# A new order for the 1224 steps of a fused gated-mix kernel

## The chip, the cores and the metric

The kernel runs on one core of a Trainium2 chip. The metric is the time of one execution on the device, in microseconds (us). The kernel before was timed in three runs; their median is the time before.

## The reference

The input x has 2048 rows of 512 float32 values. Two branches work on it and a gate mixes them:

```python
x = A_x
g = _sigmoid((x * gate_w).sum(-1, keepdims=True))
a = _A_ref(x, A_wqkv, A_w_phi, A_wo)
b = _B_ref(x, B_w1, B_b1, B_w2)
return g * a + (1 - g) * b
```

Branch A is linear attention with 32 heads of width 16. From `x @ wqkv` come q, k and v. Per head, q and k are multiplied by `w_phi`, and the feature map is the softmax of the product beside the softmax of its negative. `kv` is the sum over rows of (features of k) times v, `z` the sum over rows of the features of k. The output of a head is `num / den`, with `num` the features of q times `kv` and `den` the features of q times `z`, and the joined heads are multiplied by `wo`:

```python
phi_k = jnp.concatenate([_softmax(pk, axis=-1), _softmax(-pk, axis=-1)], axis=-1)
kv = jnp.einsum("bhsf,bhsd->bhfd", phi_k, v)
z  = jnp.einsum("bhsf->bhf", phi_k)
num = jnp.einsum("bhqf,bhfd->bhqd", phi_q, kv)
den = jnp.einsum("bhqf,bhf->bhq", phi_q, z)[..., None] + 1e-6
```

Branch B is a dense layer of width 1376 with a Mish activation, `h * tanh(softplus(h))`, and a second dense layer back to 512.

## The kernel before

Three kinds of work, by the letter that begins a step's name. **A0 to A7** are eight chunks of 256 rows: the projections to q, k and v, the features of k, and the sums `kv` and `z`. **S0 and S1** are two halves of 1024 rows of the first dense layer: five pairs of 128 hidden columns each (`_0` to `_4`) and one last group (`uf0`, `uf1`). **B0 to B3** are four blocks of 512 rows: the features of q, `num` and `den`, the second dense layer (`dn0` to `dn10`, `df`), the product with `wo`, the mix, and the output.

Every float32 factor is split into a high and a low part, so that a product is three matmuls, and one step named `h`, `hi`, `wa`, `wc`, `gh` or `xh` (ScalarE writes the high part) goes before a step named `o`, `lo`, `wb`, `wd`, `gl` or `xl` (GpSimd, or VectorE for three of the S halves' parts, subtracts to get the low part).

The v and q projections of chunks A1 to A7 and the five pairs of S0 and S1 use a scheme with seven products in the place of eight. It ties the engines together in a chain on PSUM banks. `p1` opens bank a; `c1` (ScalarE) copies it out; `p6` adds to the same bank, so it has to wait until `c1` has read it; `c6` copies again, `p7` adds, `a7` (VectorE) reads, `p4` adds, and `mA1` or `e4` (ScalarE) reads the end. `p5` opens bank b, `c5` (ScalarE) copies, `p3` adds, `a3` (VectorE) reads. `p2` opens bank c, `a2` (VectorE) reads it. Each `p` is six matmuls of 128x512. There are 17 such groups (seven chunks, ten pairs), and so 68 places where a product waits until the copy of what its bank held before has been read out: `p1` to `p6`, `p6` to `p7`, `p5` to `p3` and `p7` to `p4`.

```python
            def p6():
                product(ps["a"], sv(0, 0), Xv("2"))
...
            def copy(n, b):
                v[n] = k2("act", "hl")
                act(v[n], ps[b])
```

PSUM has eight banks in three rings: three of tag `a` (the helper `psum`, line 133), four of tag `dn`, one of tag `kv`. A step that opens a bank waits until the last reader of the bank's earlier tenant is done. Buffers in SBUF are shared in the same manner by tag.

The order of all steps is written out: `RUN` is a text of 1224 names, and `run` (line 218) calls the functions of each name in turn. Every instruction is pinned (`tc.keep_in_program_order`), so each engine and each DMA queue gets its instructions in the order in which `RUN` names their steps; between engines only semaphores order the work. A step that issues a load or a store puts it on the queue of SyncE (SP), apart from the running sums `z` of branch A, which are accumulating DMAs that GpSimd issues, and one half of the last output, which ScalarE issues. The queue of SP is in order too: a store that waits for its data holds back every load named behind it.

ScalarE holds one table of functions at a time. Exp (steps `E`, `ge`) and Mish (steps `mA0` to `mB1`, `mi0`) are in different tables, so each change from one to the other in the order of ScalarE costs an ACT_TABLE_LOAD; copies need none.

The last steps of the kernel are `fi0` to `fi3` of B3. `fi3` is split: the function `rest` (line 1038) makes the last two groups of columns of row tile 3 in two halves of 256, and stores each half on a queue of its own.

Lines that the prediction names: 118 (all matmuls), 138 (all of ScalarE's activations), 285 and 287 (the two subtractions ahead of an exp, steps `d0` and `d1`), 740, 743 and 746 (`a2`, `a3`, `a7` of the pairs), 954 (`T`, the product of the features of q with `z`), 958 (`D`, its sum), 700 (`wd`), 824 (`lo`), 559 (`gl`), 549 (the loads `lg` of the second layer's weights), 1050 and 1061 (the additions that finish an output tile).

Of the kernel before, what the change touches and what calls it, by code (L numbers as in the profile page):

```python
# [46 lines left out]
    A0.st0 A0.st1 A0.z1 A1.c6 A0.z0 A1.z0 S0.h21 A2.c1 A1.p5 A0.kv A1.c5 A1.S1 A1.rS1 A1.p7 A1.p3 A2.sh A2.sl A3.su A2.mn0 A1.ml1 A1.a7 A2.mx1 A1.st1
    A3.k1 A2.a2 A1.a3 A2.mx0 A2.d10 A2.d00 A3.p1 A2.E0 A2.S0 A3.ldx A2.rS0 A1.z1 S0.wr_0 A2.p6 A2.c6 A2.ldx A2.p5 A2.c5 A2.p7 A1.p4 A2.d01 A2.mn1
    A2.d11 A2.E1 A2.p3 A3.sh S0.wa_0 A2.ml0 A1.st0 A3.mn1 A3.c1 A3.k0 A2.a3 A2.z0 A2.st0 A3.sl A3.p5 A2.a7 A2.p4 A1.e4 A3.xh A2.S1 A3.mx0 A3.mx1
    A3.mn0 A1.kv A3.xl S0.l12 A2.e4 A2.rS1 A2.ml1 A2.kv A3.d00 A3.d10 A3.E0 S0.wb_0 S0.ws_0 A3.p6 A4.p1 A2.z1 A3.d11 A3.S0 A3.rS0 A3.ml0 A2.st1 A2.wx  # L50
    A3.c5 A4.k0 A4.mn0 A3.c6 A4.su A3.p3 A4.d10 A3.a3 A4.c1 A3.p7 A4.sh A4.mx0 S0.h11 A4.d00 A3.a7 A4.k1 A4.E0 A3.st1 A3.d01 A4.mn1 A4.d11 A4.S0 A4.sl
    A3.p2 A3.a2 A4.mx1 A4.p5 A4.p6 A3.z0 A3.E1 A4.xh A4.c6 A4.ldx A3.S1 A3.rS1 A4.p2 A4.p7 A4.d01 A4.c5 A3.ml1 A3.p4 A4.a7 A4.st1 A4.E1 A3.st0 S0.o11
    A4.xl A4.rS0 A4.ml0 A4.p3 A5.su A5.sh A4.a3 A3.z1 S0.t1 A3.e4 B0.lq0 A5.k0 A5.k1 A5.mx0 A4.S1 A4.z0 A4.rS1 A4.ml1 A5.sl S0.h1 S0.o1 A4.z1 S0.o21
    A5.xh A5.p1 A5.c1 A3.kv A5.p5 A5.c5 A4.st0 A4.a2 A5.mn0 A5.p6 A5.mx1 A5.xl A5.d01 S0.wc_0 A5.mn1 A5.d10 A5.d11 A5.d00 A5.E0 A4.p4 A5.S0 A5.rS0
# [20 lines left out]
    B0.iz2 B0.ol0 B1.S1 B0.iz0 B0.iz1 B0.wo0 B1.mi0 B1.hi0 B1.lo0 B0.iz3 B0.wo1 B1.S0 B1.rS0 B1.m0 B1.la4 B1.hc B1.la5 B1.hi1 B1.dn0 B1.mn3 B1.rS1
    B0.nu1 B1.T1 B1.de0 B1.d03 B1.D1 B1.m1 B1.d13 B1.de1 B1.d02 B1.lo1 B1.E3 B1.d12 B0.fi0 B1.rd0 B1.sc0 B1.es0 B1.cd B2.lq0 B1.hi3 B1.lo3 B0.oh1
    B1.dn1 B1.rd1 B0.ol1 B0.wo2 B1.sc1 B1.E2 B1.es1 B1.S2 B1.hi2 B1.lo2 B1.hi4 B1.lo4 S1.l11 B1.tr1 B1.dn2 B2.lq1 S1.h11 S1.o11 B1.hi5 B1.la6 B1.lo5
    S1.t1 B1.dn3 B1.dn4 B1.tr0 B1.hi6 B1.la7 B1.hi7 B0.fi2 B1.lo6 B1.rS2 B2.mx0 B1.S3 B1.la9 B0.wo3 B1.lo7 B1.T2 B1.mv0 B1.D2 B1.dn5 B1.dn6 B1.dn7
    B1.m2 B1.nu0 B1.rS3 B1.T3 B1.D3 B1.m3 B1.la8 B1.gl B1.de2 B1.ge B1.de3 B1.rd2 B1.sc2 B1.rd3 B1.es2 S1.l22 B1.sc3 B1.es3 B1.hi8 B1.lo8 B0.fi1 S1.h1
    S1.t3 S1.o1 B1.dn8 B1.gg B1.oh0 B1.tr2 B2.mx1 B1.hi9 B1.la10 B1.tr3 S1.h3 B1.lo9 B0.fi3 S1.h22 B1.ol0 B1.wo1 B1.wo0 S1.o22 B1.hi10 B1.lo10 B1.mv1  # L80
    S1.o3 B1.dn9 B1.nu1 B1.ag1 B1.df2 B1.ag0 S1.wr_0 B2.mn1 S1.t2 B2.d11 B2.d01 B2.E1 S1.wa_0 S1.fr0 B1.oh1 B2.lq2 S1.fh0 B2.S1 B1.ol1 B1.df1 S1.h2
    B1.df0 S1.wb_0 S1.p1_0 S1.c1_0 S1.ws_0 S1.wc_0 B2.d00 S1.o2 S1.l21 S1.h21 S1.wd_0 S1.o21 B2.mn0 B2.d10 B1.wo3 B1.ag3 B1.wo2 S1.fl0 S1.t4 S1.p6_0
    S1.wr_1 S1.p5_0 S1.c6_0 B2.mn2 B2.d12 B1.df3 B1.fi3 B2.rS1 B1.fi1 S1.p2_0 B2.mx2 B1.ag2 S1.a2_0 S1.wr_2 S1.c5_0 S1.p3_0 S1.p7_0 S1.a3_0 B2.E0
    B2.S0 S1.wa_1 S1.wb_1 S1.p1_1 S1.ws_1 S1.h4 S1.mB0_0 S1.o4 S1.wc_1 S1.c1_1 S1.wd_1 B1.fi0 S1.uf0 S1.a7_0 S1.p2_1 S1.p4_0 B2.rS0 S1.a2_1 B1.fi2
    B2.gr S1.p5_1 B2.mi0 B2.hi0 S1.p6_1 S1.mA0_0 B2.gl B3.lq1 B2.lo0 S1.mA0_1 B2.hc B2.dn0 B2.mn3 S1.sB0_0 B2.hi1 B2.mx3 B2.d02 B2.T0 S1.c6_1 B2.T1
    B2.D1 B2.m1 B2.de1 S1.wa_2 B2.rd1 B3.lq0 S1.p7_1 S1.mB1_0 S1.wb_2 S1.p1_2 S1.mA1_0 S1.sB1_0 B2.D0 B2.cd B2.d03 S1.c5_1 S1.p3_1 B2.E2 B2.ge B2.lo1
# [1148 lines left out]
```

## Time and profile before

| | |
|---|---|
| three runs | 435.71, 430.99 and 432.29 us |
| median | 432.29 us |
| span of the profiled execution, first to last instruction | 431.1 us |
| TensorE (PE) busy | 422.3 us, 98% |
| VectorE (DVE) busy | 369.3 us, 86% |
| ScalarE (ACT) busy | 253.6 us, 59% |
| GpSimd (POOL) busy | 263.6 us, 61% |
| mean granted clock of TensorE | 0.996 |

The profiled execution has no time of its own beside its span; the fastest of the three runs (430.99 us) is within 0.2 us of that span, so little lies around it. In the profile, a line such as L118 is a line of the kernel, `out<-in` names the tiles that an instruction writes and reads, `x12` is a count, and what stands in brackets behind a row of the timeline is the idle time of that engine before it and what ended it. A busy PE is not a PE at its peak, since the ends of matmuls are modelled; the rate is read from the starts.

### The profile page before, as it was taken

Reading aid. Unit: us, or ns where it says so; the run is one execution under the profiler, and the core shown is the slowest. Engines: PE = TensorE matmul, PEld = TensorE weight load, DVE = VectorE, ACT = ScalarE, POOL = GpSimd, SP = SyncE. Lnnn points to the kernel's source line nnn. Section 1 sums busy time; section 2 is a strip of 40 time slices with the busy share of each in tenths; the row PEclk is TensorE's granted clock in tenths of the full one; section 3 lists DMA queues with packets and bytes.
Section 4 is the critical chain, followed back from the end, with each engine's and each line's share of the span. In section 5 each row is a group of like instructions: output and inputs, shape, how many; then the busy total and the mean of one; then the engine's idle time right before and its main releaser. Section 6 shows DMA issues by size and latency. Waiting matters only on the chain. (4 is left out here: it accounts for less than half of the span.)

```text
span 431.1 us, 7558 instructions
## 1 busy us (share of the span) xinstructions
PE 422.3 (98%) x2772; PEld 340.2 (79%) x2772; DVE 369.3 (86%) x519; ACT 253.6 (59%) x373; POOL 263.6 (61%) x186
## 2 busy tenths in 40 slices
PE   8999999999998999899999999999999999999996
PEld 7888888888886877688878687788788887877875
DVE  3899789998998999998999998799989699999512
ACT  3574463646254899768679813467978467851131
POOL 2298868799674966635666494977455627541220
PEclk9999999999999999989999999999999999999999
DMA  7900597675988344433888477833533725555532
GB/s 260 366 34 28 164 273 182 140 179 126 209 171 214 108 134 123 160 109 122 235 249 281 165 239 237 281 91 122 177 119 143 232 73 188 179 199 168 197 121 75
DMA packets 52670, 74.06 MB, mean 172 GB/s; under 512 B 8085, under 2 KB 32149, under 8 KB 52633
## 3 DMA queue, kind: packets, MB, share of 16 engines
q1 hardware_dynamic: 50440, 66.36, 47.9%
q0 software_dynamic: 1904, 6.82, 9.5%
q8 instruction: 22, 0.36, 0.3%
q10 hardware_dynamic: 288, 0.39, 0.3%
q14 instruction: 16, 0.12, 0.1%
HBM read 43.53 MB, written 28.85 MB: 168 GB/s over the span
## 5 line engine op out<-in xcount | busy, mean ns | idle before, releaser
L118 PE MATMUL down<-w2g,h 128*128 128x512 f32 x316 | 98.5, 393 | 0.0
L118 PEld LDWEIGHTS down<-w2g,h 128*128 128x128 f32 x316 | 58.6, 188 | 14.8 <-issue 2.5
L118 PE MATMUL down<-w2g,l 128*128 128x512 f32 x158 | 61.8, 391 | 0.2 <-POOL l L824 0.2
L824 POOL TENSOR_TENSOR l<-act,h 128x512 fp32r<-128x512 f32 (+1 forms) x24 | 32.3, 1345 | 41.2 <-ACT h L138 16.7
L824 POOL TENSOR_TENSOR l<-actb,h 128x512 fp32r<-128x512 f32 x20 | 29.0, 1451 | 38.3 <-ACT h L138 20.7
L138 ACT ACTIVATE E<-E 128x1024 f32<-128x1024 f32 x32 | 33.4, 1057 | 16.5 <-DVE E L285 7.1
L118 PE MATMUL up<-x,w1sh 128*128 128x512 f32 x144 | 39.7, 397 | 2.2 <-DVE act L740 2.1
L118 PE MATMUL wo<-woh,ohl 128*128 128x512 f32 x128 | 40.9, 389 | 0.0
L118 PEld LDWEIGHTS down<-w2g,l 128*128 128x128 f32 x158 | 29.6, 188 | 7.5 <-POOL l L824 1.2
L118 PEld LDWEIGHTS up<-x,w1sh 128*128 128x128 f32 x144 | 26.7, 189 | 9.2 <-DVE act L740 2.5
L700 POOL TENSOR_TENSOR w1sl<-w1r,w1sh 128x1024 fp32r<-128x1024 f32 x9 | 22.2, 2467 | 18.0 <-ACT w1sh L138 17.4
L118 PE MATMUL proj<-tw,sx 128*128 128x512 f32 x126 | 31.5, 394 | 1.5 <-ACT qs L138 1.5
L628 POOL TENSOR_TENSOR x<-xr,x 128x1024 fp32r<-128x1024 f32 x10 | 26.7, 2666 | 3.6 <-ACT x L138 3.6
L118 PEld LDWEIGHTS proj<-tw,sx 128*128 128x128 f32 x126 | 23.3, 188 | 6.9 <-ACT qs L138 1.9
L138 ACT ACT_TABLE_LOAD x22 | 28.2, 1283 | 0.4
L118 PEld LDWEIGHTS wo<-woh,ohl 128*128 128x128 f32 x128 | 24.0, 188 | 5.0
L138 ACT ACTIVATE act<-act,b1s 128x512 f32<-128x512 f32 x30 | 21.4, 719 | 10.9 <-DVE act L740 4.1
L118 PE MATMUL up<-x,w1d 128*128 128x512 f32 x108 | 27.7, 398 | 0.0
L267 POOL TENSOR_TENSOR xl<-xraw,xh 128x512 fp32r<-128x512 f32 x14 | 18.3, 1370 | 15.3 <-ACT xh L138 15.0
L138 ACT ACTIVATE act<-up 128x512 f32<-128x512 f32 x30 | 17.6, 590 | 16.8 <-PE up L118 16.4
L138 ACT ACTIVATE h<-actb 128x512 fp32r<-128x512 f32 x20 | 12.4, 628 | 24.4 <-DMA actb<-ab 18.9
L118 PE MATMUL wo<-wol,ohl 128*128 128x512 f32 x64 | 24.9, 389 | 0.0
(173 smaller groups left out, 1086.4 us busy)
## 6 DMA issues: line engine op xcount, KB each, us to landing
ed<-E SPq DMA_DIRECT2D x16, 512.0 KB, 3.1
eT<-ed SPq DMA_DIRECT2D x64, 128.0 KB, 3.2
za<-E POOLq DMA_DIRECT2D x11, 512.0 KB, 6.8
xr<-in_xT_dram SPq DMA_DIRECT2D x20, 256.0 KB, 4.2
ab<-act SPq DMA_DIRECT2D x20, 256.0 KB, 2.9
actb<-ab SPq DMA_DIRECT2D x20, 256.0 KB, 3.3
pqd<-qs SPq DMA_DIRECT2D x16, 256.0 KB, 5.8
pq<-pqd SPq DMA_DIRECT2D x16, 256.0 KB, 3.6
```

Source lines behind the costliest of these rows:

```text
L118: return pin(nc.tensor.matmul(*a, **k))
L138: return pin(A_.activation(out_, in_, fn, **k))
L267: pin(eng.tensor_sub(xs[c][1][j], kt(rawx[c], SC)[:, 2 * j : 2 * j + 2, :], f32(xs[c][0][j])))
L628: pin((V if n in LOV else G_).tensor_sub(X[n][:, 1024:], xr[n], f32(X[n][:, :1024])))
L700: pin(G_.tensor_sub(W["sl"], W["r"], f32(W["sh"])))
L824: pin(G_.tensor_sub(U[i]["l"][:n, :], U[i]["a"][:n, :], f32(U[i]["h"][:n, :])))
```

## The change

The text `RUN` is replaced by another with the same 1224 names in another order. No function, tile, size or instruction changes. What moves is the place of each step in the queue of its engine, the place of each DMA in its queue, and with the order of first use also which buffer and which bank a tile gets. The names are in groups on lines that have no meaning. The lines that the prediction speaks of:

```diff
--- before.py
+++ after.py
 RUN = """
-    A0.mx0 A0.mx1 A0.xh A0.xl A0.v0 A0.mn1 A0.mn0 A0.fq A0.fh2 S0.l11 A0.d10 A0.tA0 A0.fh1 A0.v1 A0.tA1 A0.tH1 A0.fl1 A0.tB1 A0.tB0 A0.fl2 A1.p1
...
-    A6.ml1 S0.h2 S0.t3 S0.fh0 S0.t4 A7.k0 S0.h22 A6.z1 S0.fl0 S0.o22 A6.e4 A7.mn0 A6.a3 A5.kv A6.kv A7.c1 S0.lg1 A7.d10 A7.mx0 A7.d00 B0.d00 A6.zm
-    S0.o2 A7.p5 A7.E0 A7.S0 A7.rS0 A6.st0 A7.c5 A7.k1 A7.mx1 A7.mn1 S0.gh1 S0.gl1 S0.wr_1 S0.h3 S0.p1_0 A7.d01 A7.p6 A7.c6 A7.d11 A7.p3 A7.ml0 A7.E1
...
-    B0.d12 B0.dn2 S0.wd_2 B0.T0 B0.hi3 B0.D1 B0.lq3 S0.c1_2 S0.p6_2 S0.mB1_1 B0.rS0 B0.E2 B0.D0 S0.wa_3 B0.lo3 S0.sB1_1 S0.a2_2 B0.rS1 B0.m1 B0.mx3
-    S0.p4_1 S0.mA1_1 B0.hi4 S0.lg2 S0.c6_2 B0.de1 S0.wr_4 B0.dn3 S0.gl3 S0.wb_3 S0.mA0_2 S0.p5_2 S0.p1_3 S0.lg4 S0.c5_2 S0.a3_1 B1.lq0 S0.gh4 B0.lo4
...
-    B0.hi6 S0.wc_4 B0.tr0 B0.lo6 B0.dn6 S0.mB1_3 S0.sB1_2 S0.wd_4 S0.a3_3 S0.mA1_3 S0.mB0_3 S0.sB0_3 B0.T3 B0.D3 B0.S3 B1.d00 B1.lq1 S0.gl4 B0.rS3
-    S0.c1_4 B0.hi7 B1.mn0 B1.d10 S0.p6_4 S0.c6_4 B0.m2 S0.p5_4 B0.mv0 S0.p7_4 B0.de2 B0.lo7 S0.c5_4 B1.E0 B0.gg S0.h12 S0.fr1 B0.m3 B0.de3 S0.p2_4
...
-    B3.hi9 B3.lo9 B3.dn8 B3.de2 B3.rd2 B3.hi10 B3.sc2 B3.lo10 B3.es2 B3.tr3 B3.tr2 B3.mv1 B3.df1 B3.fi1 B3.nu1 B3.oh1 B3.df2 B3.ol1 B3.wo2 B3.ag2
-    B3.fi2 B3.wo3 B3.ag3 B3.df0 B3.fi0 B3.fi3
+    A0.xh A0.mn0 A0.mx1 A0.d01 A0.v0 A0.fq A0.fh1 A0.mn1 A0.d11 A0.ve0 A0.xl A2.lx A0.tA0 A0.tA1 A0.ldx A0.tH1 A0.tL1 A0.mx0 A0.d00 A0.fl1 A0.v1 A0.tB1
...
+    A6.rS1 A6.ml1 A6.z0 A5.kv S0.o1 A6.p5 A6.c5 A6.p7 A6.p3 A6.a7 S0.l22 S0.t3 A6.zr A6.z1 A7.sh A7.sl S0.lg1 A6.a3 A6.st0 A7.k0 S0.wc_0 A7.mn0 A7.d10
...
+    A7.p5 A7.k1 A7.mx1 A7.mn1 A7.d01 S0.gh1 S0.gl1 A7.p6 A7.c5 A7.p3 S0.h22 A7.d11 A7.c6 A7.p7 S0.o22 A7.E1 A7.a2 S0.fl0 S0.wr_1 S0.wa_1 S0.p1_0 S0.c1_0
...
+    A7.zt B0.d03 S0.p5_1 B0.hi0 B0.lo0 B0.dn0 S0.c5_1 S0.p3_1 S0.wb_2 S0.p2_2 B0.mn1 S0.mA1_0 B0.hi2 S0.lg3 S0.gh3 B0.lo2 A7.st1 S0.wr_3 A7.zf S0.c6_1
+    B0.gl B0.ge B0.mx1 B0.d01 S0.ws_2 B0.d11 B0.lq2 B0.mn2 B0.mx2 S0.wc_2 S0.p7_1 B0.E1 S0.a7_1 A7.zs S0.wa_3 A7.zl B1.lq3 S0.wr_4 S0.p1_2 S0.c1_2
+    S0.lg2 S0.a3_1 B0.dn3 S0.mB1_1 B0.dn2 S0.a2_2 S0.mA0_2 S0.p4_1 S0.wd_2 S0.p5_2 S0.mB0_1 S0.mB1_0 S0.sB1_0 S0.wb_3 S0.p6_2 B0.d13 B0.T0 B0.D0
...
+    B1.mx0 B0.E3 S0.wd_4 S0.p5_4 S0.mA0_3 S0.mB0_3 S0.sB0_3 B1.mn0 B0.S3 S0.c1_4 B1.d00 S0.p6_4 B0.T3 B0.D3 S0.p4_3 B0.hi7 B1.d10 S0.ldo1 B0.lo7 B0.rS3
+    B0.dn7 B0.S2 S0.gh4 B0.rS2 B0.m2 B0.de2 B0.rd2 S0.o12 B1.E0 B1.T0 B1.D0 S0.a2_4 S0.c6_4 S0.p7_4 S0.mA1_3 B0.hi8 S0.fr1 B0.lo8 B1.lq1 B1.mn1 B1.d11
+    S0.c5_4 S0.p3_4 S0.gl4 B0.dn8 S0.fh1 S0.fl1 B0.m3 B0.de3 B0.rd3 S0.mA0_4 B0.hi9 S1.l11 S1.h11 S0.ldo0 S0.mB1_3 S0.sB1_3 S0.a7_4 S0.mB1_4 S0.sB1_4
...
+    B3.ol0 B3.wo0 B3.hi7 B3.lo7 B3.dn7 B3.la9 B3.hi9 B3.ge B3.gg B3.wo1 B3.ag1 B3.la10 B3.hi10 B3.lo10 B3.cd B3.nu1 B3.dn8 B3.oh1 B3.ol1 B3.ag0 B3.wo3
+    B3.ag3 B3.lo9 B3.df0 B3.fi0 B3.df1 B3.fi3 B3.fi1 B3.wo2 B3.df2 B3.ag2 B3.fi2
 """
```

More of the change, by code (lines that the diff above doesn't have):

```diff
@@ L47 @@
[L47 to L54, printed above, removed]
@@ L75 @@
[L75 to L82, printed above, removed]
@@ L83 @@
[L83 to L86, printed above, removed]
@@ L91 @@
-    S1.ws_4 B2.rS3 B2.rS2 S1.wd_3 S1.p6_3 S1.h12 S1.c6_3 S1.fr1 S1.mA1_2 B2.lo5 S1.wc_4 S1.wd_4 B2.dn5 B2.hi6 S1.p5_3 S1.c5_3 S1.p7_3 B2.m3 S1.p1_4
-    S1.c1_4 B2.de3 B2.rd3 S1.a7_3 B2.lo6 S1.ldo0 B2.gg B3.d01 B2.hi7 B3.d11 S1.p3_3 S1.fh1 B2.T2 S1.a2_4 S1.mA0_4 B2.dn6 B3.d10 B3.mx0 S1.p6_4 S1.c6_4
-    B2.lo7 S1.p4_3 S1.fl1 B2.D2 B2.m2 B3.E1 B3.d00 B2.sc3 B2.de2 B2.rd2 B3.E0 B2.sc2 B3.lq2 B2.es2 S1.mA1_3 B2.dn7 S1.p5_4 S1.c5_4 B2.es3 S1.p7_4
-    B3.mn2 S1.ldo1 B2.hi8 S1.p3_4 B2.tr2 B3.S1 S1.WH1 S1.a3_4 S1.mB0_4 B2.lo8 B2.dn8 S1.o12 S1.mB1_3 B3.mn3 S1.sB0_4 S1.sB1_3 B2.hi9 B2.lo9 S1.a7_4
@@ new lines @@
+    B1.d02 B1.E2 B1.d03 B1.hi3 B1.lo3 B1.la2 B1.hi4 B1.lo4 B1.dn3 B2.lq0 B1.sc0 B1.es0 B1.T1 B1.D1 B1.hi2 B0.fi0 B1.tr0 B1.m1 B1.de1 B1.rd1 B1.gl B1.ge
+    B1.dn4 B1.sc1 B1.T2 B1.la7 B0.oh1 B1.S2 B1.es1 B1.tr1 B1.lo2 B1.dn2 B1.d13 B1.D2 B0.ol1 B1.E3 B0.wo3 S1.o11 B1.hi7 S1.t1 B1.rS2 S1.h1 B2.mn1 B0.wo2
+    B1.lo7 B1.dn7 B1.S3 B1.rS3 B1.la8 B1.m2 B1.de2 B1.rd2 B1.sc2 B1.T3 B1.la6 B1.la9 B1.hi9 B1.D3 B1.m3 B1.lo9 B1.dn9 B1.mv0 B1.hi5 B1.lo5 B1.dn5 B1.hi6
+    B1.lo6 B1.hi8 S1.l22 S1.h22 B1.de3 B1.rd3 B1.sc3 B1.es2 B1.tr2 B0.fi2 B1.es3 B1.tr3 B2.mx1 B2.d01 B1.dn6 S1.t3 S1.h3 B1.lo8 B2.mx0 S1.o3 B1.nu0
@@ new lines @@
+    S1.wd_1 B2.d12 B2.lq3 S1.o4 S1.p4_0 B2.hi0 B2.lo0 B2.mx3 S1.wr_2 B1.fi2 B2.S0 B1.fi1 S1.c1_1 S1.p6_1 B2.mx2 B2.gr S1.wr_3 S1.a2_1 B1.fi3 S1.p5_1
+    S1.c6_1 S1.p7_1 S1.wa_2 S1.wb_2 S1.ws_2 S1.c5_1 S1.p3_1 S1.mA0_0 S1.mA1_0 S1.p2_2 B2.hc S1.wc_2 S1.a3_1 B2.T0 B2.d02 B2.D0 B2.dn0 S1.a7_1 S1.p1_2
+    B2.hi1 B2.lo1 B2.dn1 B2.d03 B2.hi2 B2.lo2 B2.dn2 B2.E2 B2.T2 B2.D2 B3.lq0 B3.mn0 S1.mB1_1 S1.wa_3 S1.wd_2 S1.c1_2 S1.p6_2 S1.c6_2 B3.mx0 S1.a2_2
+    S1.mA0_2 S1.p5_2 S1.mB0_1 S1.sB0_1 B2.rS0 B2.m0 S1.mA0_1 B2.hi3 S1.p7_2 B2.mn3 B2.d13 B2.de0 S1.wb_3 S1.sB1_1 S1.p4_1 S1.c5_2 S1.p3_2 S1.ws_3 B2.T1
@@ new lines @@
+    B2.sc2 B2.es2 S1.fr1 B3.d11 B3.E1 B2.tr2 S1.p3_3 S1.a3_3 B3.lq2 B3.T1 S1.p6_4 B2.lo7 S1.c6_4 S1.p5_4 B2.dn7 B2.rS3 B2.m3 B2.de3 B2.rd3 S1.mB0_3
+    S1.sB0_3 B2.hi9 S1.p7_4 B2.lo9 S1.fh1 S1.fl1 B3.d00 B3.E0 S1.o12 B2.sc3 B2.es3 S1.p4_3 B2.dn9 B3.S1 B3.rS1 B2.tr3 S1.c5_4 S1.p3_4 S1.a7_4 S1.p4_4
+    S1.mB1_4 S1.sB1_4 B3.mn3 B3.D1 B3.m1 B3.de1 B3.S0 B3.la1 S1.ldo0 S1.WH1 S1.WL1 B3.rS0 B3.mx3 B3.T0 B3.D0 B3.m0 B3.de0 B2.gg S1.mA1_3 B2.hi8 S1.mA1_4
+    B2.lo8 B3.d13 B3.hi1 B3.lo1 B2.hi10 B2.lo10 S1.WH0 S1.uf1 B2.cd B2.nu0 B2.oh0 B2.ol0 B2.mv1 B2.dn8 B2.dn10 B2.iz0 B2.iz2 B3.la6 B3.gr B3.rd1 B3.mn2
@@ new lines @@
+    B3.d12 S1.a3_4 S1.mB0_4 S1.sB0_4 B3.la5 B3.mi0 B3.hc B3.la2 B3.la3 B3.rd0 B3.sc0 B3.es0 B3.tr0 B2.iz1 B3.la4 B3.d03 B3.mx2 B3.d02 S1.WL0 B2.wo0
+    B2.fi0 B3.sc1 B3.es1 B2.nu1 B3.tr1 B3.mv0 B3.E3 B3.S3 B2.wo1 B2.iz3 B2.oh1 B3.dn1 B2.ol1 B2.wo2 B2.fi2 B3.E2 B3.T2 B3.hi0 B3.lo0 B3.hi5 B3.dn0 B3.D2
+    B3.S2 B3.rS2 B3.m2 B3.de2 B3.rd2 B3.hi3 B3.lo5 B2.wo3 B2.fi3 B3.dn5 B3.lo3 B3.dn3 B3.T3 B3.hi2 B3.nu0 B3.lo2 B3.la7 B3.gl B3.dn2 B3.la8 B3.hi4
+    B3.lo4 B3.dn4 B3.hi6 B2.fi1 B3.hi8 B3.lo6 B3.dn6 B3.D3 B3.rS3 B3.m3 B3.sc2 B3.es2 B3.tr2 B3.de3 B3.rd3 B3.sc3 B3.lo8 B3.es3 B3.tr3 B3.mv1 B3.oh0
```

59 lines of the change are left out of this document (32 added, 27 removed).

## The prediction

> **What bounds the kernel now.** I read the page first, for the share of each engine; then the waits of TensorE; then stretches of time around the longest of them; then the queues that were late there.
>
> ```profile
> span 431.1 us, 7558 instructions
> PE 422.3 (98%) x2772; PEld 340.2 (79%) x2772; DVE 369.3 (86%) x519; ACT 253.6 (59%) x373; POOL 263.6 (61%) x186
> ```
>
> TensorE is busy for 422.3 of 431.1 us, and an order takes no matmul away. The chain that ended last has its rate:
>
> ```profile
> 312.57 2.72 PE down L118 x12
> ```
>
> Twelve matmuls of 128x512 start in 2.72 us, 0.227 us each, so one product `p` of six is 1.36 us and a step `dn` of twelve 2.72 us. The 8.8 us without a busy TensorE are its start, its end, and these waits:
>
> ```profile
> PE up L118 <- DVE act L740: 2.1, 1, 2.1
> PE proj L118 <- ACT qs L138: 1.5, 1, 1.5
> ...
> PE up L118 <- POOL w1sl L700: 0.3, 1, 0.3
> ...
> PE down L118 <- POOL l L824: 0.2, 1, 0.2
> ```
>
> Together 4.1 us, all behind the prologue and so within reach of a new order. The longest cost more than itself. By stretches around it (length, then busy time and count of PE, PEld, DVE, ACT, POOL, then the granted clock):
>
> ```profile
> 180.40:182.50 2.10, 0.02 (x2) 0.01 (x1) 2.10 (x4) 1.99 (x5) 1.11 (x2) 1.00 0.32 104
> 182.50:184.50 2.00, 2.00 (x6) 1.62 (x7) 1.97 (x5) 0.69 (x1) 0.82 (x1) 0.64 0.82 209
> 184.50:186.50 2.00, 2.00 (x7) 1.51 (x6) 2.00 (x6) 0.92 (x2) 0.00 (x0) 0.51 0.84 311
> ```
>
> After 2.1 us of idleness the clock was 0.64 and then 0.51: 2 x 0.36 + 2 x 0.49 = 1.7 us lost. So 4.1 + 1.7 = 5.8 us is all that better waits can bring, 1.3% of the span.
>
> [...]
>
> **The change part by part.** Both texts have the same 1224 names, so sums of work by engine stay, but for table loads (below). All steps are pinned to the text's order, so that nothing happens at all isn't a case.
>
> *The wait of 1.5 us (A7, `p6` to `p7`).* ScalarE, then TensorE:
>
> ```profile
> 137.87 0.64 ACT L138 ACTIVATE w2g<-raw 128x512 fp32r<-128x512 f32 x1 [4.12 <-DMA raw<-in_w2a_dram]
> 138.40 1.04 ACT L138 ACTIVATE x<-xr 128x1024 fp32r<-128x1024 f32 x1
> 139.53 0.60 ACT L138 ACTIVATE qs<-proj 128x512 f32<-128x512 f32 x1
> 140.18 1.66 PE L118 MATMUL proj<-tw,sx 128*128 128x512 f32 x6 [1.52 <-ACT qs L138]
> raw<-in_w2a_dram SPq DMA_DIRECT2D x6, 256.0 KB, 7.4
> ```
>
> `gh1` stood ahead of `A7.c6` in ScalarE's queue and waited 4.1 us for the load `lg1`. Loads of this kind land 7.4 us after their issue (median), and between the names `lg1` and `gh1` stand only 4.1 us of matmuls before; after the change 11.9 us (`A7.k0`, `k1` and more between). I count this wait as gone: -1.5. SP's queue isn't free of the reverse: `lg3` had 15.7 us ahead of `gh3` and has none now, and `gh3` is followed by `c6_1`. What hides it is that `p6_1` and `p7_1`, which need that copy, stand 5.9 us apart; without that cover it would cost up to 4.1 us, as above.
>
> *The wait of 2.1 us (`p5_2`).* VectorE's queue ahead of it:
>
> ```profile
> 176.86 2.31 DVE L954 TENSOR_TENSOR T<-E,zb 128x1024 f32<-128x1024 f32 x1
> 179.10 1.21 DVE L958 TENSOR_REDUCE Dn<-T 128x64 f32<-128x1024 f32 x1
> ...
> 180.69 1.15 DVE L958 TENSOR_REDUCE Dn<-T 128x64 f32<-128x1024 f32 x1
> 181.77 0.67 DVE L740 TENSOR_TENSOR act<-up,act 128x512 f32<-128x512 f32 x1
> ```
>
> `a2_2`, which frees the bank, stood behind `T0`, `D1` and `D0` of block B0, about 4.7 us of work. In the new text it follows `a3_1` at once, `T0` and `D0` come behind it, and five steps of matmuls stand between `p2_2` and `p5_2`. Gone, with its clock: -3.8. The waits of 0.3 and 0.2 us I count as gone too: -0.5.
>
> *The banks of the seven-product groups.* What is new is how close `p6`, `p7`, `p3` and `p4` stand behind the product whose copy they wait for. Of the 68 places, 10 had a single product (1.36 us) between before; now 25 have. What such a place leaves over is seen in chunk A4, where `p6`, `p2`, `p7` follow each other:
>
> ```profile
> 82.16 1.52 PE L118 MATMUL proj<-tw,sx 128*128 128x512 f32 x6
> ...
> 83.72 1.09 ACT L138 ACTIVATE qs<-proj 128x512 f32<-128x512 f32 x2 [2.25 <-PE proj L118]
> ...
> 84.88 0.84 PE L118 MATMUL proj<-tw,sx 128*128 128x512 f32 x3
> ```
>
> `p6` ends at 83.68, the copy begins at 83.72, takes 0.6 (two overlapped ones 1.09) and ends at about 84.3; `p7` starts at 84.88, in turn and unhurried. About 0.5 us is left: a ScalarE that is free holds the pace, one that is 0.6 us late does not. Of the 10 places before, one was late, by 1.5 us. The same share of 25 would be 2.5 places, 3.75 us; none late is 0. The cause of the one was a late load ahead of the copy, which got a longer lead, and the five close places of `p7` to `p4`, which wait for VectorE, all lie in the A chunks, where its operations read one operand from PSUM and keep their time (rows below). I take one late place: +1.5, with 0 and 3.75 as ends.
>
> *A pile on ScalarE (`c1_4` to `c5_4`).* Table loads rise from 22 to 24 by the order of Exp and Mish, 2.6 us on an engine that is 59% busy: hidden, except where they pile up ahead of a copy. Between `c1_4` and the end of `c5_4` the new text has `hi7`, `gh4` (two), a table load, `E0` of B1, `c6_4`, a table load, `mA1_3`, `hi8` and `c5_4` itself:
>
> ```profile
> L138 ACT ACTIVATE E<-E 128x1024 f32<-128x1024 f32 x32 | 33.4, 1057 | 16.5 <-DVE E L285 7.1 <-PE proj L118 5.3 <-DVE E L287 3.4
> L138 ACT ACT_TABLE_LOAD x22 | 28.2, 1283 | 0.4
> L138 ACT ACTIVATE act<-act,b1s 128x512 f32<-128x512 f32 x30 | 21.4, 719 | 10.9 <-DVE act L740 4.1 <-DVE act L746 4.0 <-DVE act L743 2.5
> L138 ACT ACTIVATE act<-up 128x512 f32<-128x512 f32 x30 | 17.6, 590 | 16.8 <-PE up L118 16.4 <-ACT h L138 0.4
> L138 ACT ACTIVATE h<-act 128x512 fp32r<-128x512 f32 (+2 forms) x28 | 17.6, 627 | 2.3 <-DMA ab<-act 1.3 <-PE down L118 0.7
> ```
>
> In the same sequence, with 0.64 for each `gh`: 0.63 + 1.28 + 1.28 + 1.06 + 0.59 + 1.28 + 0.72 + 0.63 + 0.59 = 8.1 us, or 7.3 with the overlap of 0.1 between neighbours. TensorE has `p6_4`, `p4_3`, `dn7` and `p7_4` in that time: 1.36 + 1.36 + 2.72 + 1.36 = 6.8 us, then `p3_4` needs `c5_4`. The wait is 0.5 us if `c1_4` ends as `p6_4` begins, 1.3 without overlap, 0 if ScalarE runs ahead by half a us. I take +0.6.
>
> *The end.* Before, the last product was split:
>
> ```profile
> 427.74 0.48 DVE L1050 SCALAR_TENSOR_TENSOR io<-rest,og_sb,io 128x256 f32<-128x256 f32 x1 [0.23 <-PE rest L118]
> 426.34 0.74 DVE L1061 SCALAR_TENSOR_TENSOR io<-down,og_sb,io 128x512 f32<-128x512 f32 x1
> out_dram<-io SPq DMA_DIRECT2D x15, 256.0 KB, 2.3
> out_dram<-io ACTq DMA_DIRECT2D x1, 128.0 KB, 1.7
> ```
>
> Now `fi3` with its halves lies ahead of `wo2`, and the kernel ends with `df2`, `ag2`, `fi2`: an addition of full width, 0.74 in place of 0.48, and a store of 256 KB, 2.3 in place of 1.7: +0.9 (0.3 if the store lands as fast as the half did). `ag2` (one copy on ScalarE) is hidden under `df2`, 1.36 us.
>
> **The sum.** 431.1 - 5.8 + 1.5 + 0.6 + 0.9 = 428.3 us for the profiled execution. It stands 1.2 below the median of the three runs; the runs differ by their waits, and part of these go, so I carry half of it over: 428.3 + 0.6 = 428.9, said as 429.0 us, 0.8% under the median.
>
> **The rivals.** *All waits go and the close places hold.* 431.1 - 5.8 + 0.9 + 0.6 (carried over) = 426.8 us. For it: nine of ten close places held. Against it: the place at `p3_4`, and 15 more close places.
>
> *VectorE's backlog comes back elsewhere.* It is busy for 86% and its operations are the same. Then the wait of 2.1 us and its clock return at another place; only 1.5 + 0.5 go: 431.1 - 2.0 + 0.6 + 0.9 = 430.6, with the whole 1.2 431.8 us. No change that can be measured. For it: VectorE was busy for all of the 2.1 us in which TensorE waited (2.10 of 2.10 in the first stretch). Against it: freeing steps now stand ahead of the long ones.
>
> *Long operations fall ahead of close places: slower.* A VectorE operation that reads two operands from SBUF lengthens beside GpSimd:
>
> ```profile
> 169.39 2.50 POOL L700 TENSOR_TENSOR w1sl<-w1r,w1sh 128x1024 fp32r<-128x1024 f32 x1 [0.31 <-PE up L118]
> 169.55 3.43 DVE L954 TENSOR_TENSOR T<-E,zb 128x1024 f32<-128x1024 f32 x1
> L287 DVE TENSOR_TENSOR E<-mn,pq 128x512 f32<-128x512 f32 x16 | 18.5, 1158 | 0.1
> L287 DVE TENSOR_TENSOR E<-mn,proj 128x512 f32<-128x512 f32 x16 | 10.8, 681 | 0.2
> ```
>
> The same subtraction takes 1158 ns from SBUF (`pq`) and 681 from PSUM (`proj`), and `T` beside a GpSimd operation of 2.50 took 3.43, 2.2 more than the 1.21 of `D`, an operation of its width. Which one is lengthened changes with the neighbours, so an order whose copies fit by half a us can be late wherever a long pair now falls: through an exp that waits for a lengthened subtraction, or a Mish that waits for a late `a2`, ScalarE's queue stops, and the copy behind it. Each such place costs 2.2 - 0.5 = 1.7 us. The time is over 1% above the median from 436.6 - 426.8 = 9.8 us on, six late places of 25; seven give 426.8 + 11.9 = 438.7 us. Against it: before, two lost more than 1 us in the whole kernel.
>
> [...]
>
> **How the numbers follow.** The forecast has 0.38, with 427 to 431 as its own range (close places between 0 and 3.75, the pile 0 to 1.3). All waits gone 0.28; the backlog elsewhere 0.15; slower 0.19. About 1% is what a measurement of this kernel can tell from no change, below 428.0 or above 436.6 us. Faster: 0.26 of the 0.28 and 0.10 of the forecast's 0.38, 0.36. Slower: 0.18 of the 0.19. The same: the rest, 0.46. The range of 8 in 10 goes from 425.5, a little under the case with all waits gone, since the three runs scatter, to 434.5, which takes in the forecast, the backlog, and the slower case up to three or four late places.
>
> **What would show it.** The waits of TensorE have no row of `up` for VectorE's L740 over 1 us and none of `proj` for ScalarE over 1; the mean clock rises from 0.996 to 1.0. Rows of `up` or `proj` for ScalarE of 0.3 to 1.5 us appear, one of them at `p3_4` around 205 to 210 us. The span ends some 4.3 us behind the start of the first operation after the last matmul, in place of 3.4 (431.1 - 427.74). I am wrong if TensorE's idle time after the prologue is more than 5 us, or if a wait of 2 us brings the half clock back.

## The result, and the profile after

The new order is slower by 5.7%: 457.26 us (median of four runs, 455.5 to 459.8) beside 431.64 for the kernel before on the same chip, a ratio of 1.057 (95% interval 1.051 to 1.064). The forecast was 429.0 us. The ratios, here and below, leave out the slowest executions of a kernel and so differ a little from the ratio of two medians. The profiled execution took 459.8 us, 1.7 more than its span. Every execution of the runs below takes 1.7 to 2.1 us more than its span too, so the span of 431.1 us before stood for some 432.8 us, near the median, and not for the fastest run.

The page of after, its busy times:

```profile
span 458.1 us, 7542 instructions
...
PE 427.5 (93%) x2772; PEld 339.7 (74%) x2772; DVE 396.8 (87%) x519; ACT 256.3 (56%) x375; POOL 266.4 (58%) x186
```

The span grew by 27.0 us. TensorE does the same 2772 matmuls in 5.2 us more and is now without work for 30.6 us in place of 8.8. VectorE does the same 519 instructions and needs 27.5 us more for them (396.8 for 369.3). ScalarE and GpSimd need under 3 us more.

What TensorE waited for in after (total, times, longest):

```profile
PE up L117 <- ACT act L137: 7.6, 5, 2.3
PE wo L117 <- DVE ohl L1011: 5.7, 4, 1.8
PE up L117 <- DVE act L745: 4.7, 3, 1.7
PE up L117 <- DVE act L739: 2.0, 1, 2.0
PE proj L117 <- ACT qs L137: 1.7, 1, 1.7
PE kvp L117 <- DVE E L301: 1.3, 1, 1.3
...
PE down L117 <- POOL l L823: 0.9, 1, 0.9
```

Lines stand one lower than before. By steps these are 19 waits with 24.8 us, from `A3.p3` at 76 us to `B2.wo2` at 410, the longest 2.3. Two are followed by half clock, each for 3.4 us, which loses 1.7 us each time. Here is the first of the two, by stretches as in the prediction:

```profile
187.00:189.00 2.00, 1.65 (x7) 1.38 (x8) 2.00 (x2) 1.86 (x4) 1.11 (x1) 0.95 0.19 73
189.00:191.00 2.00, 2.00 (x7) 1.54 (x6) 2.00 (x2) 0.00 (x0) 2.00 (x2) 0.50 0.00 0
```

VectorE's own groups, shapes apart, first before and then after:

```profile
L285 DVE TENSOR_TENSOR E<-pq,mx 128x512 f32<-128x512 f32 x16 | 15.8, 986 | 0.1
L285 DVE TENSOR_TENSOR E<-proj,mx 128x512 f32<-128x512 f32 x16 | 10.8, 682 | 0.4 <-PE kvp L118 0.2
L962 DVE SCALAR_TENSOR_TENSOR den<-Dn 128x32 f32<-128x32 f32 x16 | 4.2, 267 | 0.2
L854 DVE COPY zr<-zr 32x32 f32<-32x32 f32 x3 | 0.5, 171 | 0.1
```

```profile
L284 DVE TENSOR_TENSOR E<-pq,mx 128x512 f32<-128x512 f32 x16 | 22.1, 1389 | 0.2
L284 DVE TENSOR_TENSOR E<-proj,mx 128x512 f32<-128x512 f32 x16 | 11.0, 685 | 0.2
L961 DVE SCALAR_TENSOR_TENSOR den<-Dn 128x32 f32<-128x32 f32 x16 | 8.6, 536 | 0.4
L853 DVE COPY zr<-zr 32x32 f32<-32x32 f32 x3 | 2.7, 897 | 0.0
```

The subtraction that reads PSUM (`proj`) is as long as before. The same one from SBUF (`pq`) grew, and so did even operations that are 32 columns wide. Single rows of after:

```profile
189.14 2.81 POOL L699 TENSOR_TENSOR w1sl<-w1r,w1sh 128x1024 fp32r<-128x1024 f32 x1
189.65 2.38 DVE L976 TENSOR_TENSOR Dn<-Dn,Sm 128x64 f32<-128x64 f32 x1
...
216.57 2.40 POOL L627 TENSOR_TENSOR x<-xr,x 128x1024 fp32r<-128x1024 f32 x1
216.65 2.87 DVE L284 TENSOR_TENSOR E<-pq,mx 128x512 f32<-128x512 f32 x1
...
222.54 1.06 ACT L137 ACTIVATE E<-E 128x1024 f32<-128x1024 f32 x1 [5.01 <-DVE E L286]
223.50 0.58 ACT L137 ACTIVATE act<-up 128x512 f32<-128x512 f32 x1
...
224.13 0.74 PE L117 MATMUL up<-x,w1sh 128*128 128x512 f32 x2 [1.94 <-ACT act L137]
```

and the same two steps (`B0.m0`, `B1.d00`) before:

```profile
184.88 0.16 DVE L977 TENSOR_TENSOR Dn<-Dn,Sm 128x64 f32<-128x64 f32 x1
...
210.28 0.68 DVE L285 TENSOR_TENSOR E<-pq,mx 128x512 f32<-128x512 f32 x1
```

A product of 64 columns took 2.38 us in place of 0.16, ending just behind a GpSimd operation. `B1.d00` took 2.87 in place of 0.68; the exp behind it kept ScalarE waiting for 5.0 us, of which 2.2 are this lengthening, and the copy `c6_4`, queued behind that exp, let TensorE wait for 1.9 us at `p7_4`. Counted over all of VectorE's instructions, against the lower quartile of like ones in both traces, 34 are more than 0.2 us too long before and 47 after, and only 10 steps are among both. The excess is 32 us before and 55 after. So the length of such an operation goes with what GpSimd does at that moment and not with the step, and the lengths seen in the order of before didn't carry over to the new one.

The tail: the last addition starts at 454.19, the span ends 3.9 us later (3.4 before).

```profile
454.19 0.75 DVE L1060 SCALAR_TENSOR_TENSOR io<-down,og_sb,io 128x512 f32<-128x512 f32 x1 [3.02 <-ACT io L137]
```

### The profile page after: what moved, and what is told of

The parts are those of the page before. It is cut to its first block, busy times and chain, and to the rows that moved or that the text cites. A ratio compares the mean times of both kernels' runs of the same rounds, so it can differ in the third digit from the quotient of the medians.

```text
span 458.1 us, 7542 instructions
## 1 busy us (share of the span) xinstructions
PE 427.5 (93%) x2772; PEld 339.7 (74%) x2772; DVE 396.8 (87%) x519; ACT 256.3 (56%) x375; POOL 266.4 (58%) x186
## 4 chain that ended last, share of the span: by engine, by line
PE 48%; DVE 34%; issue 7%; POOL 5%; DMA 3%; ACT 2%; SPq 1%; DVEq 0%; POOLq 0%; ACTq 0%
PE proj L117 21%; PE down L117 10%; PE up L117 7%; PE wo L117 6%; DVE T L953 3%; DVE E L301 3%; DVE Dn L957 2%; DVE E L284 2%; DVE Sm L290 2%; DVE E L286 2%; DVE Dn L976 2%; DVE E L968 2%; DVE den L961 2%; DVE mn L274 1%; PE kvp L117 1%
## 5 line engine op out<-in xcount | busy, mean ns | idle before, releaser
L117 PEld LDWEIGHTS down<-w2g,h 128*128 128x128 f32 x316 | 59.6, 190 | 14.7 <-issue 2.3
L823 POOL TENSOR_TENSOR l<-act,h 128x512 fp32r<-128x512 f32 (+1 forms) x24 | 36.1, 1504 | 57.4 <-ACT h L137 39.0
L823 POOL TENSOR_TENSOR l<-actb,h 128x512 fp32r<-128x512 f32 x20 | 30.3, 1516 | 39.2 <-ACT h L137 18.3
L117 PE MATMUL wo<-woh,ohl 128*128 128x512 f32 x128 | 42.2, 395 | 5.8 <-DVE ohl L1011 5.7
L117 PEld LDWEIGHTS up<-x,w1sh 128*128 128x128 f32 x144 | 26.5, 188 | 14.3 <-ACT act L137 8.4
L699 POOL TENSOR_TENSOR w1sl<-w1r,w1sh 128x1024 fp32r<-128x1024 f32 x9 | 24.0, 2662 | 13.7 <-ACT w1sh L137 13.7
L266 POOL TENSOR_TENSOR xl<-xraw,xh 128x512 fp32r<-128x512 f32 x14 | 19.9, 1486 | 17.9 <-ACT xh L137 15.4
L117 PEld LDWEIGHTS up<-x,w1d 128*128 128x128 f32 x108 | 20.4, 192 | 12.6 <-DVE act L745 6.0
L301 DVE TENSOR_TENSOR E<-E,Sm 128x1024 f32<-128x1024 f32 x18 | 26.0, 1449 | 0.4
```

The source lines that it names most:

```text
L117: return pin(nc.tensor.matmul(*a, **k))
L266: pin(eng.tensor_sub(xs[c][1][j], kt(rawx[c], SC)[:, 2 * j : 2 * j + 2, :], f32(xs[c][0][j])))
L301: pin(eng.tensor_mul(hv(d["E"][:, :]), hv(d["E"][:, :]), d["S"][:, :, None].to_broadcast([P, 2 * H, DH])))
L699: pin(G_.tensor_sub(W["sl"], W["r"], f32(W["sh"])))
L823: pin(G_.tensor_sub(U[i]["l"][:n, :], U[i]["a"][:n, :], f32(U[i]["h"][:n, :])))
```

## The experiments

My theory: VectorE's operations that are lengthened beside GpSimd's reads cost the 27 us. The rivals: the close places of TensorE's order, or the queue order itself, would cost it at normal durations too; or GpSimd's own lengthened operations. "Order of before" and "order of after" are the two texts of `RUN`; each ratio is to runs of the kernel before on the same chip. The rows come from several chips, on which the kernel before had medians of 428.7 to 431.6 us, so medians of different rows compare to some 2 us only.

| kernel | median, us | ratio to before (95%) |
|---|---|---|
| order of before, no reads | 427.7 | 0.997 (0.993 to 1.001) |
| order of after, no reads | 428.3 | 1.000 (0.998 to 1.003) |
| after to `S0.p1_1`, then before | 436.7 | 1.020 (1.013 to 1.028) |
| before to `S0.p1_1`, then after | 459.9 | 1.074 (1.068 to 1.081) |
| order of after, no reads, longer GpSimd | 457.4 | 1.065 (1.059 to 1.070) |
| order of after, no reads, 39 us more on VectorE | 456.2 | 1.062 (1.056 to 1.068) |
| order of before, the same | 444.5 | 1.036 (1.030 to 1.041) |
| order of after, no reads, 19 us more | 435.9 | 1.017 (1.011 to 1.024) |
| order of before, the same | 429.1 | 1.004 (0.999 to 1.008) |
| order of after, VectorE relieved of 33 us | 445.0 | 1.041 (1.032 to 1.050) |
| order of before, the same | 430.8 | 1.004 (1.000 to 1.009) |
| order of after, ten GpSimd operations quiet | 449.7 | 1.041 (1.036 to 1.046) |
| order of after, both | 434.1 | 1.008 (1.005 to 1.011) |
| three orders with queues exchanged | 511, 528, 536 | 1.18, 1.22, 1.24 |
| order of before, two cures, first try | 441.5 | 1.027 (1.023 to 1.032) |
| order of before, two cures, second try | 427.0 | 0.994 (0.991 to 0.997) |

**GpSimd without reads.**

```diff
+        def thin(fn, o, a, b):
+            c = (slice(None),) * (len(o.shape) - 1) + (slice(0, 8),)
+            pin(fn(o[c], a[c], b[c]))
+            pin(nc.gpsimd.memset(o.bitcast(F32), 0.0))
+            return nc.gpsimd.memset(o.bitcast(F32), 0.0)
...
+        def tensor_sub(o, a, b):
+            return G_.thin(nc.gpsimd.tensor_sub, o, a, b)
```

GpSimd's additions go through `thin` in the same way, but for those that make the mask at the start. The memsets write the whole result, the eight columns too, so these results hold zeros.

> The order of before; each GpSimd subtraction or addition is cut to its first 8 columns and followed by two memsets of the whole result, so GpSimd is about as busy (264 us before) but reads next to nothing from SBUF. What it leaves out: the low parts, the pair sums of x and one addition of zacc hold zeros but for 8 columns. My theory (VectorE's operations with two SBUF operands lengthen beside GpSimd's reads) expects VectorE's busy time to fall from 369 to about 340 us and the time to about 425 to 430, since the order of before has only 4 us of waits. The rivals (close places of the products, or a bad queue order on VectorE and ScalarE) expect the same small gain here.

> The same replacement in the order of after; it leaves out the same parts. My theory expects VectorE's busy time to fall from 397 to about 340 us, as in the order of before, TensorE's idle time from 30.6 to under 12, and the time from 457 to 425 to 433, within 4 us of the order of before without reads. If the close places of the products or the queue order are the cause by themselves, the waits stay: 445 us or more, 15 us or more above the order of before without reads.

Both are in their ranges. The order of after comes out at 428.3 us, 0.6 above the order of before, and 29 under its own time with the reads. VectorE is busy for 337.9 us in the order of before and 344.8 in that of after. The page of the order of after and its waits behind the prologue:

```profile
PE 419.7 (98%) x2772; PEld 339.3 (80%) x2772; DVE 344.8 (81%) x519; ACT 256.1 (60%) x375; POOL 244.4 (57%) x510
```

```profile
PE proj L138 <- POOL sx L125: 0.6, 1, 0.6
PE proj L138 <- POOL xl L125: 0.6, 1, 0.6
```

```profile
L305 DVE TENSOR_TENSOR E<-pq,mx 128x512 f32<-128x512 f32 x16 | 10.9, 686 | 0.2
```

No wait for ScalarE or VectorE is left, with all 25 close places in the text, and `E<-pq,mx` takes the 686 ns of its PSUM twin. The close places and the queue order cost nothing while operations keep their length: both rivals of that kind fall. GpSimd's 244 us fit its real work less its own lengthening (266 less some 22 over the medians of like operations), so the stand-in is about as long as that work unlengthened. But GpSimd's lengthening is gone too, which leaves that rival open here.

**GpSimd without reads, but slower.** A third memset for each operation.

> As the order of after without GpSimd's reads, but with three memsets for each of its operations: about 1.7 us for a 512-column result where the two took about 1.15 and the real subtraction 1.3 to 1.45, so GpSimd is slower than in after but still reads next to nothing. The same parts are left out. If the loss of after comes from lengthened VectorE operations: still about 429 (427 to 435). If the two memsets helped because GpSimd was done sooner: back towards 440 or more.

```profile
PE 431.2 (95%) x2772; PEld 343.5 (75%) x2772; DVE 345.2 (76%) x519; ACT 256.3 (56%) x375; POOL 339.4 (74%) x672
```

```profile
PE proj L139 <- POOL sx L126: 10.5, 4, 5.5
```

457.4 us, a miss, and no answer: three memsets made GpSimd 73 us busier than in after, and TensorE waited for GpSimd itself in the A chunks, for 10.5 us on `sx` where after has none. VectorE kept 345 us, and the waits of after (`wo` for `ohl`, `up` for `a7`) are absent. It shows only that GpSimd has no 73 us to spare.

**Halves of the two orders.** `RUN` is one text to the step `S0.p1_1`, and then what is left in the sequence of the other.

> The order of after up to the first product of the second pair (S0.p1_1, about 155 us), then all remaining steps in the order of before. In the trace of after 3.5 of the 24.8 us of waits lie before this place. If lengthened operations depend on the neighbours at hand and not on a lasting backlog: about 432 + 3.5 = 435 (433 to 440). If the A part of the new order leaves VectorE with a backlog that never clears: 445 or more.

> The order of before up to S0.p1_1, then the remaining steps in the order of after. With 21.3 of the 24.8 us of waits and both half-clock stretches of after behind this place: about 432 + 22 = 453 (446 to 460) if the rest carries its own waits; under 440 if the waits of the rest come from the backlog of the A part.

436.7 and 459.9 us, both in the range, the second at its upper end. Each part brings a loss of its own, +6.6 and +29.8 against the 430.1 of before, and the second is no smaller for an A part in the old order: no backlog that the one hands on to the other is needed for it. The two add up to 36.4 us where the whole new order lost 25.6, so the loss of a part depends on what stands beside it.

**Fixed extra work on VectorE, no reads.**

```diff
-                pin(V.tensor_mul(d["T"], d["E"], B["zb"]))
+                for _ in range(2):
+                    pin(V.tensor_mul(d["T"], d["E"], B["zb"]))
...
-            at(key, f"es{t}", lambda d=d: scale_by(d, V))
+            at(key, f"es{t}", lambda d=d: (scale_by(d, V), scale_by(d, V)))
```

> The order of after without GpSimd's reads (two memsets), and each of the 16 products T and the 16 scalings es of the B blocks done twice on VectorE: 32 operations of 1.21 us, 39 us of fixed extra work, between the 32 us that the lengthened operations add in before and the 55 us in after. It leaves out the same parts, and scales E twice. If what costs is the sum of VectorE's work against its slack (94% busy from 180 to 260 us without reads): 440 to 455. If what costs is single operations that grow many times over at a place that nobody chose: 428 to 434.

> The same extra 39 us of VectorE work in the order of before without GpSimd's reads (VectorE 86% busy from 180 to 260 us). The sum theory expects 430 to 438, less than in the order of after by 8 us or more; the theory of single long operations expects 427.5 to 431.

The half dose has the first of the two edits alone.

> The order of after without GpSimd's reads (the low parts, pair sums and one sum left out as before) and each T done twice: 19.4 us of fixed extra VectorE work, half of the earlier dose, which cost 28 us. If every us beyond a small slack costs about a us: 437 to 446. If the slack holds half of the dose: under 434.

> The same half dose in the order of before, where the full dose cost 17 us: 429 to 436, and less than in the order of after by 5 us or more if the order of before has the more slack on VectorE.

The order of after loses 7.6 us by the half dose and 27.9 by the full one (435.9 and 456.2 less 428.3), the order of before 1.4 and 16.8 (from 427.7). By the ratios, which allow for the chips, these are 7.3 and 26.5, and 2.9 and 16.6 us. Two of the sum theory's four ranges were missed by about 1 us, and that of the full dose in the order of before by 6.5. So added VectorE time is enough to make a loss of this size, without GpSimd's reads, and it makes it for the most part at the same places:

```profile
PE wo L138 <- DVE ohl L1033: 8.0, 3, 4.3
PE up L138 <- DVE act L766: 6.0, 3, 2.8
PE up L138 <- ACT act L158: 3.5, 2, 2.0
```

L1033, L766 and L158 are `ol`, `a7` and ScalarE's copies, the first three rows of the waits of after; eight of the waits stand at the very steps of after (`S0.p1_4`, `p7_4`, `p3_4`, `p4_4`, `B0.wo3`, `S1.p4_2`, `S1.p4_4`, `B2.wo2`). The order of after holds less: without reads VectorE is busy in it for 75.5 of the 80 us from 180 to 260, in the order of before for 69.1. The theory of irregular single operations, which expected no loss here, is wrong as the whole of it. But the sum alone doesn't decide either: the order of before, which holds its own 32 us of lengthening at no cost that can be measured (0.997), loses 16.8 by 39 us at places of my choice.

**VectorE relieved, GpSimd whole.**

```diff
-                pin(V.tensor_reduce(d["D"], hv(d["T"][:, :]), axis=AX.X, op=ALU.add))
+                pin(V.tensor_reduce(d["D"], hv(d["T"][:, :])[:, :, :2], axis=AX.X, op=ALU.add))
...
-                pin(V.transpose(d["E"][:, :], d["E"][:, :]))
+                pin(V.transpose(d["E"][:, :128], d["E"][:, :128]))
```

> The order of after with GpSimd's work whole, and VectorE relieved of work that is never lengthened: the 16 sums D read 2 of their 16 features, and the 16 transposes of E take 128 of 1024 columns, about 33 us less on VectorE. It leaves out the rest of these sums and transposes. If VectorE's load against its slack is the cause of the loss, the time falls from 457 to 428 to 436 although GpSimd and its reads are untouched; if GpSimd's own lengthened operations (about 25 us) or another queue are the cause, it stays above 445.

> The same relief in the order of before, which leaves out the same parts. Both theories expect little, since only 4.1 us of waits and 1.7 of clock are there to be had: 424.5 to 430.

445.0 us, at the border that I had drawn for "another cause". In the order of before the same relief brings no gain, 430.8 us, 0.8 above its range, so the 12.3 us gained here are not what 33 us less VectorE work brings anywhere. The waits for `ohl` vanish and those for `a2` and `a7` shrink to one of 0.8 us; those for ScalarE stay:

```profile
PE up L118 <- ACT act L138: 7.3, 5, 2.6
PE down L118 <- POOL l L824: 2.0, 1, 2.0
PE proj L118 <- ACT qs L138: 1.6, 1, 1.6
PE kvp L118 <- DVE E L302: 1.3, 1, 1.3
```

VectorE is now busy for 364 us, less than before the change, and TensorE still waits at `A3.p3`, `A7.kv`, `S0.p7_2`, `p7_4`, `p3_4` and `S1.p7_0`. Each of these stands behind an operation lengthened beside one of GpSimd's: `ws_0` 3.2 us beside `o21`, `ws_1` 1.6 beside `A7.z0`, `ws_3` 1.2 and 1.4 beside `gl3`, `T3` 3.4 beside `o12`, `B2.d00` 2.9 beside `S1.o21`.

**Ten GpSimd operations quiet.** The same stand-in as above, for eight steps only.

```diff
+    QUIET = "S0.o21 A7.z0 S0.wb_3 S0.gl3 B0.lo7 S0.o12 S1.wd_0 S1.o21".split()
```

> The order of after with 10 of GpSimd's 186 operations made to read next to nothing (8 columns, then two memsets), those that ran beside the lengthened VectorE operations ahead of the waits that the relief of VectorE left over: S0.o21, A7.z0, S0.wb_3, S0.gl3, B0.lo7, S0.o12, S1.wd_0, S1.o21. It leaves out these ten results. If single long VectorE operations cause those waits (A3.p3 1.7, A7.kv 1.3, S0.p7_2 2.3 with 1.7 of clock, S0.p7_4 1.9, S0.p3_4 1.5, S1.p7_0 1.4), 11.8 us go: about 445 (440 to 450). If not, 455 to 459.

> Both together: VectorE relieved of 33 us of sums and transposes, and the same 10 GpSimd operations quiet; it leaves out what the two leave out. If the backlog and the single long operations are the two parts of the loss: 430 to 437. If something else holds the 16 us that the relief left: 441 to 446.

Alone they give back 7.6 us (449.7 for 457.3), in the range, short of the 11.8 expected: the waits at `A3.p3`, `A7.kv`, `S0.p7_2` and `S1.p7_0` are gone and `p7_4` has 0.4 left, but the 1.5 at `p3_4` stay, and 1.8 us come up at `S0.p5_3`. With the relief the time is 434.1 us, which gives back 23.2 of the 29.0 us between the order of after and the same without reads (by the ratios 21 of 25). So the loss has two parts: a VectorE that falls behind, and single long operations ahead of an exp, a `wc` or a Mish that hold ScalarE's queue. The 5.8 us left are waits at `p3_4`, `p4_4`, `B1.dn1` and `S1.p4_2`, which I didn't follow further. GpSimd's own lengthening holds 2.0 us of them at most (`B1.dn1`, `l`); that it plays a part in the rest isn't excluded, but 176 of its 186 operations were whole.

**Queues exchanged.** One engine's steps take their place from one text, the others' from the other, and the steps are merged by their data and buffers.

> TensorE's queue as in after (92% of neighbouring steps in after's sequence, 19 of after's 25 close places), VectorE's as in before (98%), ScalarE's and GpSimd's for the most part as in before (84%, 86%). If the close places of the products cost the time: 445 to 460. If it is VectorE's queue that takes on more than it can hold: 430 to 440.

> The reverse: TensorE's queue as in before (93%, 9 close places), VectorE's as in after (98%), ScalarE's and GpSimd's for the most part as in after (87%, 83%). If the close places cost the time: 430 to 440. If it is VectorE's queue: 446 to 462.

> VectorE's queue alone as in after (96%), TensorE's (98%), GpSimd's (98%) and ScalarE's (93%) as in before. If VectorE's sequence by itself carries the loss: 445 to 460. If it takes the meeting of VectorE's and GpSimd's new sequences: 430 to 440, with about as much lengthening as before (VectorE busy 365 to 375).

510.8, 527.9 and 536.4 us, far above all that was expected, and no answer. TensorE idles for 63 to 78 us in them, at waits on every engine. None of these mixed orders fits its queues, so they don't tell which engine's sequence costs what.

**The two cures alone, in the order of before.** First try, `lg1` ahead of `A6.a7`, and second, behind `A6.st1`; in both:

```diff
-    ... S0.wd_2 B0.T0 B0.hi3 B0.D1 B0.lq3 S0.c1_2 S0.p6_2 S0.mB1_1 B0.rS0 B0.E2 B0.D0 S0.wa_3 B0.lo3 S0.sB1_1 S0.a2_2 B0.rS1 ...
+    ... S0.wd_2 B0.hi3 S0.c1_2 S0.a2_2 B0.T0 B0.D1 B0.lq3 S0.p6_2 S0.mB1_1 B0.rS0 B0.E2 B0.D0 S0.wa_3 B0.lo3 S0.sB1_1 B0.rS1 ...
```

> The order of before with the two cures that the prediction counted, and nothing else: the load lg1 named in chunk A6, about 8 us earlier, and a2_2 with its copy c1_2 moved ahead of T0, D1 and D0 of block B0. The prediction's terms: 1.5 + 3.8 us gone, 0.987 of the time of before, if no other wait takes their place. If lengthened operations decide which wait shows, others appear in their place: 0.995 to 1.01.

441.5 us, a miss by both terms:

```profile
PE up L118 <- DVE E L302: 11.5, 1, 11.5
```

```profile
142.75 0.69 DVE L285 TENSOR_TENSOR E<-pq,mx 128x512 f32<-128x512 f32 x1 [11.02 <-DMA zacc<-E]
```

SP's queue in the same kernel, and then in before (`lg1` issues two loads):

```profile
116.55 0.60 SPq L549 DMA_DIRECT2D raw<-in_w2a_dram  x1
...
129.13 0.33 SPq L549 DMA_DIRECT2D raw<-in_w2a_dram  x1
129.55 1.29 SPq L489 DMA_DIRECT2D zacc<-za  x1
```

```profile
117.57 0.35 SPq L489 DMA_DIRECT2D zacc<-za  x1
...
129.48 1.39 SPq L549 DMA_DIRECT2D raw<-in_w2a_dram  x2
```

The first of the two loads went 13 us earlier (116.55; 129.48 before). The second was hardly earlier for its earlier name (129.13; 129.91 before): it can't go before its buffer is free. While it waited it held the read-back `zr` behind it for 12 us; the accumulation of the z sums waited for that, and VectorE for the buffer of E that the accumulation reads, 11 us. Named behind `zr`, the two loads go at 123.50 and 129.00:

> The two cures again, with the load lg1 named behind the read-back of the z sums on SP's queue instead of ahead of it (ahead of it, it held that queue, and with it VectorE, for 11 us). The prediction's terms: 5.3 us gone, 425 where before has 430.4. If lengthened operations take over: 428 to 434.

```profile
PE 420.0 (99%) x2772; PEld 338.7 (80%) x2772; DVE 365.8 (86%) x519; ACT 253.5 (60%) x373; POOL 264.1 (62%) x186
```

427.0 us, 0.6% (0.3 to 0.9) faster than before and the fastest kernel here that computes the whole. Its profiled span is 425.8 us, 5.3 less than that of before, and no wait behind the prologue is over 0.3 us. The time lies between the two ranges that were named, 425 and 428 to 434.

## Why the prediction was wrong

*What better waits can bring (5.8 us).* Right in kind: two cures of 5.3 us by the prediction's terms took 5.3 us off the span and 3.5 off the median. That the span agrees to a tenth is luck in part, since single executions of the kernel before range from 426.5 to 433.8 us on that chip.

*The waits of 1.5 and 2.1 us gone (-1.5, -3.8, -0.5).* Gone at their own places; after has no wait at `A7.p7` or `S0.p5_2`. The prediction wanted no row of `up` for VectorE's `a2` over 1 us and none of `proj` for ScalarE over 1: both are there again, at `S0.p1_4` (2.0) and `A3.p3` (1.7). The mean clock was to rise from 0.996 to 1.0 and fell to 0.993.

*The banks of the seven-product groups (+1.5).* This is the step that failed, together with a premise of the whole sum. The step looked for lateness at the 25 close places; of the 19 waits two stand there, `S0.p7_2` and `S1.p7_0`, with 3.8 of 24.8 us, and without GpSimd's reads none does. The premise is "sums of work by engine stay": VectorE's time was put at no change, though the prediction's own rows of `T` showed that its lengths weren't fixed. VectorE needed 396.8 us in place of 369.3, the excess of its operations rose from 32 to 55 us, and the doses show that the order of after can't hold even 19 us for nothing.

*The pile at `p3_4` (+0.6).* A wait was there (1.5 us, at 227), but the pile alone doesn't make it: without reads the same pile leads to no wait. It stays, at 1.0 to 1.2 us, when VectorE is relieved. That it came where it was forecast is luck in part.

*The end (+0.9).* 3.9 us behind the start of the last addition in place of 3.4: +0.5, between its ends.

*The step from the span to the time (+0.6).* It should have been 1.7 us, the difference that every execution shows.

*The rival that was right in kind.* "Long operations fall ahead of close places" named the mechanism and priced a place at 1.7 us; the mean of the 19 waits is 1.3. It was too small because it let only close places be late and had no backlog of VectorE in it: products four to eight us behind the one whose copy they need (`S0.p7_4`, `S0.p4_4`, `S1.p4_2`) were late as well, and those with `wo`. Without that mechanism the rest of the sum was good: the order of after with no reads has a span of 426.6 us, and 431.1 - 5.8 + 0.9, without a late place, is 426.2. That the forecast span of 428.3 us equals the time of that kernel is chance.

Of the two signs named for being wrong, both came: TensorE idled for over 5 us behind the prologue, and waits of 2 us brought the half clock back.

## What to carry to other kernels

Where VectorE reads its operands from SBUF beside a busy GpSimd, don't carry durations measured in one order over to another: here 34 and 47 operations were lengthened in the two orders, and only 10 steps in both. Price a new order with the lengthening as a load that can fall anywhere (here some 30 to 55 us on VectorE), and ask how much of it each stretch holds: with VectorE busy for 86% of the stretch from 180 to 260 us without it the order held, with 94% it didn't. Where a trace shows a few waits by name, move a few steps by hand: here that brought 0.6% where 1.3% was the most. Each load that is moved has to be followed through all that stands behind it in its queue.
